# Strided attention and layer-norm FFN on one core: prologue and first chunk as one list of 500 small stages

## The chip, the cores and the metric

The kernel runs on one core of a Trainium2 chip. The metric is the device time of one execution in microseconds (us); the median of three runs is 963.8 us. The engines are named as the profile names them: PE is TensorE, PEld its weight loads, DVE is VectorE, ACT is ScalarE, POOL is GpSimd, SP is SyncE, whose queue issues almost all DMAs.

## The reference

Eight batches, eight heads, 576 tokens, 64 columns a head. Half of the heads look at a local band, half at every 32nd token. The result of attention (512 columns a token) goes through a layer norm without mean offset and a two-layer network with a residual. The matrices `w_ch1` and `w_ch2` come in as 64-bit floats.

```python
scores = scale * np.matmul(q, k.transpose(0, 1, 3, 2))
mask_local = (rel >= 0) & (rel < stride)
mask_strided = (rel >= 0) & (pos[None, :] % stride == pos[:, None] % stride)
scores = np.where(masks[None, :, :, :], scores, -1000000000.0)
attn = np.exp(scores - np.max(scores, axis=-1, keepdims=True))
attn = attn / (np.sum(attn, axis=-1, keepdims=True) + 1e-09)
x = np.matmul(attn, v)                        # heads side by side: [8, 576, 512]
mu, var = x.mean(-1), ((x - mu) ** 2).mean(-1)
xn = (x - mu) / np.sqrt(var + 1e-06) * g_ln
out = x + np.maximum(xn @ w_ch1, 0.0) @ w_ch2
```

## The kernel before

**Tiling.** The 8 x 576 tokens are nine chunks of 512: chunk c holds the first 512 tokens of batch c, the ninth the 64 left over of each batch. For each chunk the hidden layer is walked in 16 slices f of 128 columns. `ffn1` (L630 on) makes slice f of the hidden layer: eight matmuls with the high half of the weights (L643) and four with the low half (L647) into one PSUM bank `ph`. ACT takes the high part of the result (`hh`, L651), DVE the rest (`hl`, L652). `ffn2` (L662) then adds 12 matmuls of the slice to the outputs `po`, which hold four PSUM banks for the whole chunk. Every product is made of high and low parts, so that 24 matmuls belong to one f.

**Attention.** Two heads are a `Pair`; four pairs make a batch, in the order 2, 0, 3, 1 (2 and 3 strided, 0 and 1 local). In what follows a pair is called by its place in the list of all pairs: 0 to 3 are batch 0, 4 to 7 batch 1. For batch 0 `q` and `k` come in as rows and PE transposes them (`t_rows`, L321); from pair 4 on they come in as `raw` through many small descriptors (`load_qk`, L299) and DVE transposes them (`t_piece`, L362 to L367). Then: scores (L396), mask and row maximum on DVE (L423, L432), subtraction on POOL (L437), exponential on ACT (L440), transpose of the weights on PE (L449) and a copy (L454), product with `v` (L464), division on DVE (L475, L476, L513), store to a DRAM scratch (L522 to L527), transpose to the layout of the FFN (L536), high part on ACT (L559), low part on DVE (L561). For local pairs of batch 0 ACT makes a shifted copy of `v` (`v_shifted`, L354).

**Weight splits.** While chunk 0 runs, `Split(f)` turns the 64-bit weights of slice f into a high and a low fp32 part, once for the first matrix (i = 0) and once for the second (i = 1): `scaled` on ACT into the single PSUM tile of the pool `ps_r` (L188), `low` on DVE (L194), `magnitude` and `sign` on DVE (L198, L204); for i = 0 also the factor g on POOL (`by_g`, L212), the mean over the 512 input rows by four matmuls against a matrix of g (`column_mean`, L219) and its subtraction on DVE (`centred`, L223); then `two_parts`, ACT for the high (L234) and POOL for the low (L235). `w_load` (L170, L173) brings 1 MB per f.

**Order.** Each engine takes its instructions in the order of the program; the last loop of the kernel ties them so. Before, the prologue handles batch 0 pair by pair, then slices 0 and 1 are split whole. Then chunk 0 runs f = 0 to 15, and with each f comes the split of f + 2, spread around `ffn1` and `ffn2`, and one piece of batch 1 from the generator `pieces`. From chunk 1 on there are no splits; each f has a piece of the next batch.

Slice f of the first layer is called F(f) for L643 and H(f) for L647, the second layer G(f).

Of the kernel before, what the change touches and what calls it, by code (L numbers as in the profile page):

```python
# [19 lines left out]
def kernel(  # L20
# [43 lines left out]
    ps_o = ctx.enter_context(tc.tile_pool(name="ps_o", bufs=2, space=bass.MemoryType.PSUM))  # L64
# [115 lines left out]
    class Split:  # L180
        def __init__(self, f):
            self.f = f
            self.bits = [t.rearrange("p (f t) -> p f t", t=2) for t in staged.pop(f)]
# [42 lines left out]

        def two_parts(self, i):
            w = (self.wg, self.w[1])[i]
# [5 lines left out]
            nc.scalar.activation(out=t[:, 0], in_=w, func=AF.Copy)  # L234
            nc.gpsimd.tensor_tensor(out=t[:, 1], in0=w, in1=t[:, 0].bitcast(F32), op=ALU.subtract)  # L235

        def whole(self):
            self.low(0)
            self.scaled(0)
            self.magnitude(0)  # L240
            self.sign(0)
            self.low(1)
            self.by_g()
            self.column_mean()
            self.scaled(1)
            self.magnitude(1)
            self.sign(1)
# [635 lines left out]
```

## Time and profile before

| what | value |
|---|---|
| median of three runs | 963.8 us (962.1 to 964.55) |
| profiled execution, own time | 962.39 us |
| its span | 960.6 us |
| PE busy | 926.0 us, 96% |
| DVE busy | 427.0 us, 44% |
| ACT busy | 212.6 us, 22% |
| POOL busy | 127.3 us, 13% |
| F(0) of chunk 0 starts | 55.78 us |
| F(0) of chunk 1 starts | 177.97 us |

The span counts from the first to the last instruction; 1.79 us of the execution lie around it. Busy times of PE count pipelined matmuls whose ends are modelled, so a start-to-start distance is the better price of a matmul group. A start in the timeline is counted from the start of the span.

### The profile page before, as it was taken

The numbers are of one execution on the slowest core, as the hardware profiler recorded it, in microseconds if no ns is written. First come the engines' busy times: TensorE is split into PE (matmuls) and PEld (weight loads), VectorE is DVE, ScalarE is ACT, GpSimd is POOL, SyncE is SP. The second block draws the span as 40 slices with busy tenths as digits, with TensorE's granted clock in tenths as the row PEclk, the third lists the DMA queues.
The fourth block names the chain that finished last, engine by engine and source line by source line (L and its number), as shares of the span: only waits on it lengthen the run. The fifth ranks groups of instructions, "written<-read, shape, count | busy, mean of one in ns | idle before, by whom it ended". The sixth has DMA issues, their size and how long they took to land.

```text
span 960.6 us, 18743 instructions
## 1 busy us (share of the span) xinstructions
PE 926.0 (96%) x7936; PEld 766.6 (80%) x7936; DVE 427.0 (44%) x857; ACT 212.6 (22%) x337; POOL 127.3 (13%) x150
## 2 busy tenths in 40 slices
PE   6669999999999999999999999999999999999997
PEld 6558787788888888888888888888888888888886
DVE  2689988633454334434543454335432331132112
ACT  3534444121111121211121211121111111110100
POOL 4245556100000001000100010001000000000000
PEclk9879999999999999999999999999999999999999
DMA  9866873442333334333433344334221121002001
GB/s 200 238 158 155 208 212 78 85 101 46 86 63 94 62 85 73 95 61 85 73 95 62 83 74 96 62 64 94 71 38 48 36 76 45 0 1 88 1 1 44
DMA packets 239427, 80.16 MB, mean 83 GB/s; under 512 B 190064, under 2 KB 232688, under 8 KB 239344
## 3 DMA queue, kind: packets, MB, share of 16 engines
q1 hardware_dynamic: 236128, 77.27, 35.3%
q10 hardware_dynamic: 3216, 1.71, 0.8%
q8 instruction: 62, 1.02, 0.5%
q14 instruction: 21, 0.17, 0.1%
HBM read 59.48 MB, written 19.46 MB: 82 GB/s over the span
## 4 chain that ended last, share of the span: by engine, by line
PE 89%; DMA 3%; DVE 3%; SPq 3%; issue 1%; ACT 1%; ACTq 0%; DVEq 0%
PE po L662 40%; PE ph L643 26%; PE ph L647 13%; PE m L464 2%; PE m L396 2%; SPq L299 2%; PE cm L219 2%; PE n L449 1%; PE n L536 1%; DMA rows<-in_k_dram 1%; DMA s<-in_moe_w_ch_dram 1%; DVE p L198 1%; SPq L170 1%; PE av L464 0%; DMA raw<-in_k_dram 0%
## 5 line engine op out<-in xcount | busy, mean ns | idle before, releaser
L662 PE MATMUL po<-w,hh 128*128 128x512 f32 x1152 | 362.2, 396 | 0.0
L652 DVE SCALAR_TENSOR_TENSOR hl<-ph,hh 128x512 fp32r<-128x512 f32 x144 | 99.6, 692 | 465.7 <-ACT hh L651 465.3
L662 PEld LDWEIGHTS po<-w,hh 128*128 128x128 f32 x1152 | 211.2, 188 | 43.6
L643 PE MATMUL ph<-xh,w 128*128 128x512 f32 x576 | 227.2, 395 | 0.2 <-ACT xh L559 0.2
L643 PE MATMUL ph<-xl,w 128*128 128x512 f32 x576 | 225.7, 392 | 0.2 <-DVE xl L561 0.2
L662 PE MATMUL po<-w,hl 128*128 128x512 f32 x576 | 224.9, 391 | 0.0
L651 ACT ACTIVATE hh<-ph 128x512 fp32r<-128x512 f32 x144 | 85.9, 597 | 488.8 <-PE ph L647 488.8
L647 PE MATMUL ph<-xh,w 128*128 128x512 f32 x576 | 154.4, 390 | 0.0
L643 PEld LDWEIGHTS ph<-xl,w 128*128 128x128 f32 x576 | 109.0, 189 | 22.8 <-DVE xl L561 0.5
L643 PEld LDWEIGHTS ph<-xh,w 128*128 128x128 f32 x576 | 108.9, 189 | 22.8 <-ACT xh L559 0.7
L647 PEld LDWEIGHTS ph<-xh,w 128*128 128x128 f32 x576 | 108.5, 188 | 22.7
L662 PEld LDWEIGHTS po<-w,hl 128*128 128x128 f32 x576 | 108.1, 188 | 23.3
L437 POOL TENSOR_TENSOR sm<-sm,mx 128x648 f32<-128x648 f32 (+1 forms) x32 | 40.6, 1269 | 420.2 <-DVE mx L432 409.9
L624 POOL TENSOR_TENSOR rs<-rs,mhalf 128x1 f32<-128x1 f32 x36 | 20.0, 554 | 342.3 <-DVE rs L623 342.3
L440 ACT ACTIVATE sm<-sm 128x648 f32<-128x648 f32 (+1 forms) x32 | 23.8, 744 | 138.7 <-POOL sm L437 138.6
L219 PE MATMUL cm<-r,gmean 128*128 128x128 f32 x128 | 19.3, 299 | 16.2 <-DVE r L204 11.3
L219 PEld LDWEIGHTS cm<-r,gmean 128*128 128x128 f32 x128 | 17.7, 208 | 19.1 <-issue 15.6
L561 DVE TENSOR_TENSOR xl<-n,xh 128x480 fp32r<-128x480 f32 (+2 forms) x36 | 22.7, 666 | 15.4 <-ACT xh L559 15.4
L188 ACT ACTIVATE p<-s 128x512 f32<-128x512 f32 x32 | 20.5, 642 | 34.5 <-DVE r L204 33.1
L432 DVE TENSOR_REDUCE mx<-sm 128x12 f32<-128x648 f32 (+1 forms) x32 | 26.4, 824 | 2.3
L513 DVE TENSOR_TENSOR xo<-m,den 64x64 f32<-64x64 f32 (+3 forms) x120 | 27.1, 290 | 0.1
L235 POOL TENSOR_TENSOR w<-wg,w 128x512 fp32r<-128x512 f32 x16 | 20.7, 1292 | 41.9 <-ACT w L234 38.8
(95 smaller groups left out, 645.9 us busy)
## 6 DMA issues: line engine op xcount, KB each, us to landing
s<-in_moe_w_ch_dram SPq DMA_DIRECT2D x32, 512.0 KB
out_dram<-x SPq DMA_DIRECT2D x32, 256.0 KB
raw<-in_q_dram SPq DMA_DIRECT2D x112, 72.0 KB
raw<-in_k_dram SPq DMA_DIRECT2D x112, 72.0 KB
xds<-xo SPq DMA_DIRECT2D x32, 162.0 KB
v_l<-in_v_dram SPq DMA_DIRECT2D x32, 144.0 KB
xdl<-xo SPq DMA_DIRECT2D x16, 256.0 KB
x<-xdl SPq DMA_DIRECT2D x32, 128.0 KB
```

Source lines behind the costliest of these rows:

```text
L219: nc.tensor.matmul(self.mean, gmean[:, c, :], w[:, c, :], start=(c == 0), stop=(c == NCC - 1))
L235: nc.gpsimd.tensor_tensor(out=t[:, 1], in0=w, in1=t[:, 0].bitcast(F32), op=ALU.subtract)
L432: nc.vector.reduce_max(mx[:, :, 0:nt], sm, axis=AX.X)
L437: nc.gpsimd.tensor_tensor(out=sm, in0=sm, in1=mx[:, :, 0:nt].unsqueeze(3).broadcast_to([P, 2, nt, w]), op=ALU.subtract)
L440: nc.scalar.activation(out=sm, in_=sm, func=AF.Exp, scale=SCALE)
L513: nc.vector.tensor_tensor(out=xo[r, t0:t1, h0:h1].rearrange("p t h d -> p h t d"), in0=av, in1=den[r, h0:h1, t0:t1].unsqueeze(3).broadcast_to(
L561: nc.vector.tensor_tensor(out=dst(xl), in0=src, in1=dst(xh).bitcast(F32), op=ALU.subtract)
L643: nc.tensor.matmul(ph, w1h[:, cc], x[:, cc, :], start=(n == 0), stop=False)
L647: nc.tensor.matmul(ph, w1l[:, cc], xh[:, cc, :], start=False, stop=(cc == NCC - 1))
L651: nc.scalar.activation(out=hh, in_=ph, func=AF.Relu)
L652: nc.vector.scalar_tensor_tensor(out=hl, in0=ph, scalar=0.0, in1=hh.bitcast(F32), op0=ALU.max, op1=ALU.subtract)
L662: nc.tensor.matmul(po[i], hx[:, cs], w, start=(f == 0 and n == 0), stop=(f == NFC - 1 and n == 2))
```

## The change

Prologue and chunk 0 no longer come from loops. A table `ORDER` of some 500 words sets them one after the other; `one` takes a word such as `sg:4:0` (operation, pair or slice, part, PSUM room) and writes that stage's instructions. The stages themselves were helpers before and are now cut finer: `t_rows` and `t_copy`, `s_mask`, `s_max`, `s_sub`, `s_exp`, `v_full`, `v_den`, `v_out`, `v_store`, `x_turns`, `x_high`, `x_low`, `low`, `scaled`, `magnitude`, `sign`, `by_g`, `block_sum`, `column_mean`, `centred`, `high`, `rest`, and F, H, G of the FFN. The loops over chunks 1 to 8 stay.

Four stages change what they compute with:

- `low` of slices 2 to 15 (28 instructions) goes to ACT as `lowA`: the top byte of the low word is read, a byte in eight, scaled by 1/32 and rounded to an integer, instead of a shift by 29.
- The mean over rows: POOL adds the four blocks of the weighted slice to one (`block_sum`, two instructions), and PE makes the mean by one matmul against a constant matrix. The build of `gmean` on DVE goes.
- `by_g` writes in place, so that a split holds two buffers of the pool `tk` and not three.
- `v_shifted` goes from ACT to POOL (four copies).

```diff
+ORDER = """
+T:0:0:0 T:0:1:1 c:0:0: T:1:1:2 c:0:1: S:0::0 c:1:1: T:2:0:1 mask:0 max:0 T:1:0:2 c:2:0: sub:0
+...
+hi:1:0 sg:2:0 hi:1:1 lo:1:0 st:0 V:4::0 sc:2:1 lowA:3:1 H:0 mg:2:1 W:5 byg:2 lowA:4:0 den:4 lo:1:1
+...
-        def low(self, i):
+        def low(self, i, on_act):
             t = self.bits[i][:, :, 0]
-            nc.vector.tensor_scalar(t, t, 29, None, op0=ALU.logical_shift_right)
+            if on_act:
+                nc.scalar.activation(
+                    out=t, in_=self.top[i], func=AF.Copy, scale=1.0 / 32, bias=-31.0 / 64)
+            else:
+                nc.vector.tensor_scalar(t, t, 29, None, op0=ALU.logical_shift_right)
...
         def by_g(self):
-            w = self.w[0].rearrange("p (c f) -> p c f", c=NCC)
-            self.wg = tkp.tile([P, DM], F32, tag="tk", name=f"wg{self.f}")
...
+            self.wg = self.w[0].rearrange("p (c f) -> p c f", c=NCC)
             nc.gpsimd.tensor_tensor(
-                out=self.wgv, in0=w, in1=gcol.unsqueeze(2).broadcast_to([P, NCC, P]), op=ALU.mult)
-
-        def column_mean(self):
-            w = self.w[0].rearrange("p (c f) -> p c f", c=NCC)
-            self.mean = bank(f"cm{self.f}")[:, 0:P]
-            for c in range(NCC):
-                nc.tensor.matmul(
-                    self.mean, gmean[:, c, :], w[:, c, :], start=(c == 0), stop=(c == NCC - 1))
+                out=self.wg, in0=self.wg, in1=gcol.unsqueeze(2).broadcast_to([P, NCC, P]),
+                op=ALU.mult)
+
+        def block_sum(self):
+            nc.gpsimd.tensor_tensor(
+                out=bsum, in0=self.wg[:, 0:2], in1=self.wg[:, 2:4], op=ALU.add)
+            nc.gpsimd.tensor_tensor(out=bsum[:, 0], in0=bsum[:, 0], in1=bsum[:, 1], op=ALU.add)
+
+        def column_mean(self, ps):
+            self.mean = ps[:, 0:P]
+            nc.tensor.matmul(self.mean, mean, bsum[:, 0], start=True, stop=True)
...
-                    nc.scalar.copy(
+                    nc.gpsimd.tensor_copy(
                         out=self.v[64 * h:64 * h + 32, 1:NB, 0:D],
                         in_=self.v[64 * h + 32:64 * h + 64, 0:NB - 1, 0:D])
...
+    for word in ORDER.split():
+        part = (word.split(":") + [""] * 3)[0:4]
+        one(part[0], *(int(x or 0) for x in part[1:]))
+    prev = 0, NFC - 1, hs[NFC - 1], xres
...
+    for c in range(1, NCHUNK):
```

What the table moves is shown at three places.

PE around F(0): scores, transposes and products of attention (`pp`, `av`, `px`), the column means `cm`, and the first two matmuls of F(0) (`ph_0`). Before:

```order
L449 MATMUL pp_1_712<-ident,sm_195 128x128 x5
L219 MATMUL cm_731<-r_0_726,gmean 128x128 x4
L464 MATMUL av_1_748<-v_l_183,pt_1_718 32x65 x40
L536 MATMUL px_3_795<-ident,xo_3_701 128x128 x6
L536 MATMUL px_1_806<-ident,xo_1_791 128x128 x4
L219 MATMUL cm_837<-r_1_832,gmean 128x128 x4
L643 MATMUL ph_0_869<-xh_656,w_0_742 128x512
L643 MATMUL ph_0_869<-xl_657,w_0_742 128x512
```

And now:

```order
L490 MATMUL pp_1_705<-ident,sm_201 128x128 x5
L505 MATMUL av_711<-v_l_189,pt_1_705 32x65 x40
L271 MATMUL cm_764<-bsum,mean 128x128
L434 MATMUL s_780<-kt_s,qt_s 64x54 x24
L577 MATMUL px_811<-ident,xo_3_761 128x128 x6
L577 MATMUL px_839<-ident,xo_1_835 128x128 x4
L490 MATMUL pp_852<-ident,sm_200 128x128 x6
L271 MATMUL cm_865<-bsum,mean 128x128
L697 MATMUL ph_0_872<-xh_529,w_0_806 128x512
L697 MATMUL ph_0_872<-xl_530,w_0_806 128x512
```

The last product of batch 0 (`av`) no longer stands behind the first column mean; the scores (`s_780`) and the transpose (`pp_852`) of pair 4 stand ahead of F(0), where they stood behind it; a column mean is one matmul.

DVE in the prologue, from the first `low` on: the splits of slices 0 and 1 (`s`, `p`, `r`), divisions (`den`, `xo`), low parts of attention (`xl`) and the transposes of `raw` for pair 4. Before:

```order
L194 TENSOR_SCALAR s_0_249<-s_0_249 128x512
L198 SCALAR_TENSOR_TENSOR p_0_723<-p_0_723,s_0_249 128x512
L204 SCALAR_TENSOR_TENSOR r_0_726<-s_0_249,p_0_723 128x512
L194 TENSOR_SCALAR s_0_250<-s_0_250 128x512
L198 SCALAR_TENSOR_TENSOR p_0_736<-p_0_736,s_0_250 128x512
L204 SCALAR_TENSOR_TENSOR r_0_739<-s_0_250,p_0_736 128x512
L223 TENSOR_TENSOR wg_729<-wg_729,cm_731 128x512
L475 TENSOR_SCALAR den_201<-av_1_748 128x2x5
L476 RECIPROCAL den_201<-den_201 128x2x5
L513 TENSOR_TENSOR xo_1_791<-av_1_748,den_201 128x2x5x64
```

And now, from `sign` of slice 0 on:

```order
L254 SCALAR_TENSOR_TENSOR r_0_684<-s_0_509,p_0_635 128x512
L409 STREAM_TRANSPOSE qt_s<-raw_2_581 128x18x32
L409 STREAM_TRANSPOSE kt_s<-raw_2_581 128x18x32
L517 TENSOR_SCALAR den_206<-av_652 128x12
L518 RECIPROCAL den_206<-den_206 128x12
L244 TENSOR_SCALAR s_0_510<-s_0_510 128x512
L244 TENSOR_SCALAR s_1_677<-s_1_677 128x512
L248 SCALAR_TENSOR_TENSOR p_0_699<-p_0_699,s_0_510 128x512
L555 TENSOR_TENSOR xo_3_761<-av_652,den_206 128x2x6x64
L244 TENSOR_SCALAR s_1_678<-s_1_678 128x512
L254 SCALAR_TENSOR_TENSOR r_0_766<-s_0_510,p_0_699 128x512
L274 TENSOR_TENSOR r_0_684<-r_0_684,cm_764 128x512
```

The two transposes of pair 4 stood behind all of batch 0 and now stand among it; the split of slice 1 begins before that of slice 0 is centred.

DVE in the middle of chunk 0, one slice's worth: before, around F(4).

```order
L194 TENSOR_SCALAR s_6_924<-s_6_924 128x512
L223 TENSOR_TENSOR wg_1128<-wg_1128,cm_1212 128x512
L198 SCALAR_TENSOR_TENSOR p_6_1221<-p_6_1221,s_6_924 128x512
L204 SCALAR_TENSOR_TENSOR r_6_1232<-s_6_924,p_6_1221 128x512
L194 TENSOR_SCALAR s_6_925<-s_6_925 128x512
L652 SCALAR_TENSOR_TENSOR hl_4_1253<-ph_4_1239,hh_4_1252 128x512
L198 SCALAR_TENSOR_TENSOR p_6_1237<-p_6_1237,s_6_925 128x512
L204 SCALAR_TENSOR_TENSOR r_6_1265<-s_6_925,p_6_1237 128x512
```

And now:

```order
L248 SCALAR_TENSOR_TENSOR p_7_1247<-p_7_1247,s_7_1103 128x512
L714 SCALAR_TENSOR_TENSOR hl_4_1274<-ph_4_1223,hh_4_1263 128x512
L254 SCALAR_TENSOR_TENSOR r_7_1277<-s_7_1103,p_7_1247 128x512
L274 TENSOR_TENSOR r_6_1204<-r_6_1204,cm_1249 128x512
L248 SCALAR_TENSOR_TENSOR p_7_1290<-p_7_1290,s_7_1104 128x512
L254 SCALAR_TENSOR_TENSOR r_7_1312<-s_7_1104,p_7_1290 128x512
```

The two `low` are gone from DVE, and at `hl` of slice 4 it is in the split of slice 7, where it was in that of slice 6.

## Rows read from the trace of the kernel before

**Rows 1.** The page: busy tenths of PE and DVE in 40 slices of 24 us.

```profile
PE   6669999999999999999999999999999999999997
...
DVE  2689988633454334434543454335432331132112
```

**Rows 2.** Windows by stage: length, busy (instructions) by engine, PE clock, DMA share, GB/s.

```profile
0.00:55.78 55.78, 33.18 (x762) 29.78 (x763) 26.62 (x61) 25.24 (x33) 17.05 (x42) 0.90 0.92 213
55.78:73.02 17.24, 14.45 (x108) 11.78 (x108) 13.79 (x22) 7.31 (x13) 8.69 (x7) 0.84 0.47 141
73.02:177.97 104.95, 102.27 (x985) 83.64 (x984) 91.95 (x149) 46.23 (x77) 54.81 (x46) 1.00 0.63 156
177.97:960.60 782.63, 776.13 (x6089) 641.42 (x6087) 294.68 (x627) 133.77 (x215) 46.73 (x55) 1.00 0.29 63
```

**Rows 3.** Windows of 2 us in the prologue, the same columns.

```profile
24.00:26.00 2.00, 2.00 (x77) 1.93 (x69) 1.86 (x4) 0.22 (x2) 0.19 (x1) 1.00 1.09 387
...
42.00:44.00 2.00, 1.79 (x8) 1.78 (x8) 1.59 (x4) 0.65 (x1) 1.16 (x1) 0.50 0.60 166
...
66.00:68.00 2.00, 2.00 (x7) 1.52 (x6) 1.51 (x3) 1.98 (x4) 0.46 (x1) 0.50 0.04 12
```

**Rows 4.** Timeline of PE: start, duration, line, instruction, idle time ahead and its releaser.

```profile
42.21 2.05 PE L219 MATMUL cm<-r,gmean 128*128 128x128 f32 x8 [5.27 <-DVE r L204]
...
54.08 2.04 PE L219 MATMUL cm<-r,gmean 128*128 128x128 f32 x8 [6.06 <-DVE r L204]
55.78 0.77 PE L643 MATMUL ph<-xh,w 128*128 128x512 f32 x1
...
63.45 1.16 PE L219 MATMUL cm<-r,gmean 128*128 128x128 f32 x8 [2.79 <-DVE sm L423]
...
73.02 0.48 PE L643 MATMUL ph<-xh,w 128*128 128x512 f32 x1
...
79.79 1.05 PE L219 MATMUL cm<-r,gmean 128*128 128x128 f32 x8
80.60 0.48 PE L643 MATMUL ph<-xh,w 128*128 128x512 f32 x1
...
83.53 0.93 PE L464 MATMUL av<-v_s,pt 54*64 54x65 f32 x48
84.39 0.73 PE L662 MATMUL po<-w,hh 128*128 128x512 f32 x2
...
177.97 0.47 PE L643 MATMUL ph<-xh,w 128*128 128x512 f32 x1
```

**Rows 5.** Groups by line and shape, 73.02 to 177.97 us: busy us, mean ns, idle ahead.

```profile
L235 POOL TENSOR_TENSOR w<-r,w 128x512 fp32r<-128x512 f32 x13 | 19.1, 1466 | 0.0
L194 DVE TENSOR_SCALAR s<-s 128x512 uint32<-128x512 uint32 x24 | 19.0, 792 | 0.0
L235 POOL TENSOR_TENSOR w<-wg,w 128x512 fp32r<-128x512 f32 x13 | 16.8, 1293 | 34.8 <-ACT w L234 31.7 <-DMA s<-in_moe_w_ch_dram 3.1
L198 DVE SCALAR_TENSOR_TENSOR p<-p,s 128x512 uint32<-128x512 uint32 x24 | 16.6, 692 | 0.4 <-ACT p L188 0.4
...
L188 ACT ACTIVATE p<-s 128x512 f32<-128x512 f32 x24 | 15.4, 644 | 26.3 <-DVE r L204 25.0
...
L212 POOL TENSOR_TENSOR wg<-r,gcol 128x512 f32<-128x512 f32 x12 | 12.4, 1037 | 0.0
```

**Rows 6.** Timeline of DVE, three rows: a transpose of `raw`, and `low` twice.

```profile
49.82 1.25 DVE L367 STREAM_TRANSPOSE qt_s<-raw 128x576 f32<-128x576 f32 x1
...
51.99 0.42 DVE L194 TENSOR_SCALAR s<-s 128x512 uint32<-128x512 uint32 x1
...
92.63 1.13 DVE L194 TENSOR_SCALAR s<-s 128x512 uint32<-128x512 uint32 x1
```

**Rows 7.** Timeline of SP's queue: issue of `raw` for `k` of pair 4.

```profile
25.98 4.18 SPq L299 DMA_DIRECT2D raw<-in_k_dram  x4
```

**Rows 8.** Timeline of ACT: two shifted copies of `v`.

```profile
28.69 2.22 ACT L354 COPY v_l<-v_l 32x1088 f32<-32x1088 f32 x2
```

More of the change, by code (lines that the diff above doesn't have):

```diff
@@ L19 @@
+"""
 @with_exitstack
@@ L61 @@
     dram = ctx.enter_context(tc.tile_pool(name="dram", bufs=1, space=bass.MemoryType.DRAM))
[L64 removed]
+    ps_o = [ctx.enter_context(tc.tile_pool(name=f"ps_o{i}", bufs=1, space=bass.MemoryType.PSUM))
+            for i in range(2)]
     ps_h = ctx.enter_context(tc.tile_pool(name="ps_h", bufs=1, space=bass.MemoryType.PSUM))
@@ L75 @@
     gcol = const.tile([P, NCC], F32, name="gcol")
-    gmean = const.tile([P, NCC, P], F32, name="gmean")
+    mean = const.tile([P, P], F32, name="mean")
+    bsum = const.tile([P, 2, P], F32, name="bsum")
+    const.tile([P, P], F32, name="gap")
+    nc.vector.memset(mean, 1.0 / DM)
     mask_l = const.tile([P, 64], F32, name="mask_l")
@@ L233, in two_parts, with rest @@
                 w_pools[1].tile([P, 88], F32, name="pad")
[L234 to L247, printed above, removed]
-            self.centred()
-            self.two_parts(0)
-            self.two_parts(1)
+            nc.scalar.activation(out=t[:, 0], in_=self.w[i], func=AF.Copy)
+        def rest(self, i):
+            t = (w1s, w2s)[i][self.f]
+            nc.gpsimd.tensor_tensor(
+                out=t[:, 1], in0=self.w[i], in1=t[:, 0].bitcast(F32), op=ALU.subtract)
     banks = [(ps_a, "a", 1024)]
@@ L675, in finish, with second @@
                         out[2 * i + j, CH:S, :], x[REST * j:REST * (j + 1)])
-    WAHEAD = 2
-    banks[:] = [(ps_a, "a", 1024), (ps_o, "o", 1024), (ps_o, "o", 1024)]
+    po = None
+    def second(c, f, h, xres):
+        nonlocal po
+        if f == 0:
+            po2 = [ps_o[i].tile([P, 1024], F32, tag="o", name=f"po{c}_{i}") for i in range(NT // 2)]
+            po = [po2[i // 2][:, DM * (i % 2):DM * (i % 2 + 1)] for i in range(NT)]
+        ffn2(c, f, h, po)
+        if f == NFC - 1:
+            finish(c, po, xres)
     first = pairs[0:NHP]
@@ new lines, with room, weights, split @@
+    ps, ph, hs, splits = {}, {}, {}, {}
+    xres = [None] * NT
+    def room(name, buf):
+        pool, tag = ((ps_a, "a"), (ps_o[0], "o"), (ps_o[1], "o"))[buf]
+        ps[name] = pool.tile([P, 1024], F32, tag=tag, name=f"{name}")
+        return ps[name]
+    def weights(f):
+        if f == NF2:
+            w_late()
+        w_load(f)
+    def split(f):
+        if f not in splits:
+            splits[f] = Split(f)
+        return splits[f]
+    def residue(i):
+        xres[i] = [x_load(0, i)]
@@ L770 @@
     gen = pieces()
[L772 to L788 removed]
+    ps_r_ctx.close()
+    ps_m = ctx.enter_context(tc.tile_pool(name="ps_m", bufs=1, space=bass.MemoryType.PSUM))
+    banks[:] = [(ps_m, "m", 1536)]
+    for c in range(1, NCHUNK):
         xres = []
         tail = {}
[L791 removed]
         for f in range(NFC):
[L793 to L814 removed]
+            ph = ffn1(c, f)
+            hh = h_high(c, f, ph)
+            h = hh, h_low(c, f, ph, hh)
             if c + 1 < B:
@@ L824 @@
                         x_turn(B, i, tail[i])
-            if new:
-                new.sign(1)
-            if prev is not None:
-                second(*prev)
-            if new:
-                new.column_mean()
-            elif c == 0:
-                next(gen, None)
+            second(*prev)
             i = f - (NFC - NT - 3)
```

370 lines of the change are left out of this document (202 added, 168 removed).

## Prediction

> **What bounds the kernel now.** I read the page first [rows 1]: PE is below nine tenths only in the first four slices, some 70 us, and in the last. From 177.97 us, where chunk 1 begins, the change touches nothing and PE is the bound: 776.13 us busy of 782.63 [rows 2], the rest of it the tail. So the question is how much earlier F(0) of chunk 1 can begin than 177.97 us; what is won there is won at the end.
>
> Ahead of it I cut the time at two starts of PE, F(0) at 55.78 and F(2) at 73.02 us [rows 4]. In the prologue PE is busy for 33.18 of 55.78 us [rows 2]; its last two long gaps, 5.27 and 6.06 us, end with `sign` of slices 0 and 1 on DVE, which the column means need [rows 4]. So the prologue waits for the chain attention, then split, that DVE takes one after the other. Between F(0) and F(2) a third gap of 2.79 us ends with a mask on DVE [rows 4], and the granted clock is 0.84 [rows 2]: it reads 0.50 both behind the gap of 5.27 us and behind that of 2.79 us [rows 3]. That is 1.2 GHz in place of 2.4. From F(2) on PE is busy for 102.27 of 104.95 us and DVE for 91.95 [rows 2]. DVE is almost full there too, but PE lost only 2.7 us to it. This stage can shrink by work taken from PE, and otherwise hardly.
>
> **The change part by part.** I price three stages: the start of F(0), from there to F(2), from there to chunk 1.
>
> *Column means.* A mean of four matmuls (eight records) takes PE 0.81 us from its start to the next [rows 4]. With one matmul it should take a quarter, 0.20 us; bounds are 0 and 0.81. After F(2) there are 12 such groups before and 13 now: 9.7 less 2.6 gives 7.1 us off PE (0 to 9.7). The matmul now waits for two more instructions of POOL. They read 256 and 128 columns; against 1.04 us for `by_g` with 512 [rows 5] I take 0.9 us for both (bounds 0.4 and 2.1). That is latency of a split made more than a slice ahead, so PE pays for it only if splits run late.
>
> *POOL.* Between F(0) and chunk 1 it was busy for 8.69 and 54.81, together 63.5 us [rows 2]. With 16 block sums at 0.9 it has 78 us, at 2.1 it has 97, in a stage that I expect to last 109. It stays off the end, but its queue gets a wait in the prologue: the subtraction of pair 2 now stands behind the four shifted copies of `v`. A pair of those takes ACT 2.22 us [rows 8]. POOL has no such row; I take ACT's and allow twice that. Twice would put the subtraction, the exponential of pair 2 on ACT and the first `scaled` queued behind it up to 4.4 us later.
>
> *`low`.* DVE loses 24 of 0.79 us after F(2) [rows 5] and four more before it, some 22 us. ACT gains 28. Its nearest row is `scaled`, the same 512 elements at the same stride of 8 bytes, 0.64 us [rows 5]: 18 us more on 53.5 busy between F(0) and chunk 1 [rows 2]. A byte as input is in no row; the bounds are 0.6 and 1.1 us (one copy of 1,088 elements [rows 8]), so 70 to 84 us. It fits beside PE at either end. The Trainium skill, page "ScalarE: Activation LUTs", section "Rules for kernel authors", would leave such arithmetic on DVE, since DVE is faster per element. The rows agree in part, 0.42 us alone on DVE but 1.13 beside POOL [rows 6]. By the rule the change would free 28 times 0.42 or 11.8 us of DVE and not 22, and the sum stays as it is, because DVE at 94 us of 109 would still be off the end.
>
> With 105.7 us busy before [rows 2] less 22, DVE is near 84 of 109 us. This is what lets splits run ahead of PE.
>
> *Start of F(0).* It needs the last low part of batch 0. Now the two transposes of `raw` for pair 4 stand in DVE's queue ahead of most of batch 0's second half, so DVE stops there until `raw` has landed. Before, its issue ended at 30.2 us [rows 7], behind the weights of slices 0 and 1; now slice 1 stands behind it, and 1 MB at 387 GB/s [rows 3] is 2.7 us less. With some 3 us to land I take 31 us; bounds are 28 and 36 (nothing hidden, and POOL's 4.4 us on top). From the first transpose to the last low part there are 24 instructions on DVE. The mean of that engine from start to start is 91.95/149, 0.62 us [rows 2]: 14.8 us. F(0) comes at 45.8 us, 10 earlier. Four `low` in this stretch are priced like the rest; the spread between 0.42 and 1.13 [rows 6] is 2.8 us, which I add to the bounds: 42 to 52.
>
> The Trainium skill, page "SBUF — State Buffer", section "Who interferes with whom", says that VectorE's two-port modes, which a shift by a constant can enter, and GpSimd lock each other out. The rows agree: 1.13 us beside POOL, 0.42 without [rows 6]; and POOL's 1.47 against 1.29 us [rows 5]. By it every one of the four shifts would wait if POOL is working just then, the upper bound above.
>
> *F(0) to F(2).* One slice of 12 first-layer matmuls takes 2.93 us (80.60 to 83.53), the product for a pair 0.86 [rows 4]. The chain now is F(0) and H(0) with the product of pair 4 between, 3.8; its division and one `sign` on DVE partly beside H(0), 1.5; the transpose of pair 4, 0.6; F(1) and H(1), 2.9; G(0), also 12 matmuls, 2.9; the mean 0.2; `centred` and the high part, 0.7 and 0.6; handoffs 0.5. That is 13.7 us at full clock. PE idles in the prologue as before, so I let 0.50 [rows 3] hold for part of the first 4.4 us and add 1.3 (0 to 4.4): 15.0 us against 17.24. F(2) comes at 60.8 us against 73.02.
>
> *F(2) to chunk 1.* From 104.95 us go the 2.7 idle, 7.1 of means, and the product (0.86) and transpose (0.6) of pair 4 that now lie ahead: 93.1; I leave 0.6 for new bubbles: 93.7.
>
> *Queues.* On SP the weights of slice 4 now stand behind the store of pair 3, those of slice 2 behind a load of `v` that waits for pair 1's product. ACT's shifts for slices 2 to 4 would hold the high parts and exponentials queued behind them if these loads came late. In the stretch the DMAs are busy for 0.47 to 0.63 [rows 2] and a megabyte takes 2.7 us, so I cost it at nothing; if the cover is gone, F(0) slips by about that much.
>
> *Sum.* 45.8 + 15.0 + 93.7 = 154.5 us, against 177.97: 23.5 us less. The profiled execution took 962.39 us, 960.6 span and 1.8 around it: 938.9 us. Its time is 1.4 below the median of the runs, so against the median of 963.8 I forecast 940 us, with 934 to 947 as this case's own range.
>
> **The rivals.** *The front half does not come.* In-order holds (raw, the copies on POOL, weights behind stores) eat what attention ahead gives, and F(2) stays at 73. For it speaks that DVE's queue in the prologue now depends on DMAs in the middle of the chain; against it that DVE has 22 us less to do and long idle times in the first 56 us (26.62 busy [rows 2]). Then only 2.7 + 7.1 + 1.4 us or 11 are won: 952 us.
>
> *It comes fuller.* F(0) at 43 us, full clock from the start, PE without a bubble: 43 + 13.7 + 92.5 = 149, that is 29 us less: 935; with cheaper handoffs and short bubbles around the means gone too, 932. For it speaks PE's shorter gaps ahead of F(0): scores, two transposes and `pp` of pair 4 fill them.
>
> *The pace of the splits stays.* The single PSUM tile of `scaled` makes a chain: `scaled` 0.64, `magnitude` 0.69, `sign` alike [rows 5], twice a slice, some 4.5 us with handoffs against 5.8 us of matmuls a slice. Only if each link waits 0.6 us more in its queue does it bind, and then nothing is won behind F(2) and the front is given back: 960 to 965 us.
>
> *Slower.* The shift on ACT reads one byte in eight and writes integers in place, a form that no row shows. The stage from F(0) at 46 would have to last until 181 us, 135 us, for a loss beyond 0.3%. ACT has 53.5 us of other work there [rows 2], so the mechanism decides from (135 - 53.5)/28 or 2.9 us a shift. At 3.5 it gives some 980 us. The nearest row says 0.64, so the chance is small.
>
> **How the numbers follow.** 0.62 for the forecast, 0.17 for the front half that does not come, 0.12 for the fuller gain, 0.05 for the pace that stays, 0.04 for the slow shift. About 0.3% is what a measurement of this kernel can tell from no change. The first three are faster by more than that, and 0.02 of the fourth: 0.93. The rest of the fourth is the same, 0.03; the last is slower, 0.04. The range takes in the fuller gain and the front half that does not come, and leaves out the last two cases and the edges: 931 to 953 us.
>
> **What would show it right or wrong.** F(0) at 42 to 52 us, and the low part of pair 3 on DVE as its releaser; F(2) near 61; between F(2) and chunk 1 some 94 us with under 2 us of idle PE; a column mean of two records and about 0.2 us; DVE busy for about 84 us between F(0) and chunk 1, `scaled` and the shift on ACT equal within 0.2 us; POOL under 100 us. If F(0) comes early and chunk 1 doesn't, the splits are late: then PE's idle time names `centred` or the high part, and I have misjudged their chain. If DVE waits for a transpose of `raw` past 36 us, the prologue is wrong. Chunk 1 to the end should take 782 to 783 us as before; another number there would show an effect that I haven't named.

## The result, and the profile after

The changed kernel took 949.25 us (median of 4 runs, 949.24 to 951.44), the kernel before 963.04 beside it (962.1 to 964.55): a ratio of 0.986, 95% interval 0.984 to 0.988. The forecast was 940 us with a range of 931 to 953. So the direction and the range held, but of 23.5 us that were to be won 13.9 came: the profiled span is 946.7 us where it was 960.6.

The page of the changed kernel, busy tenths of PE and DVE in 40 slices (before: [rows 1]):

```profile
PE   7689889999999999999999999999999999999997
...
DVE  3877676433543355334543344345433321122112
```

PE is at eight tenths or less in the first six slices but one, where it had been full from the fourth slice on. The same by stage, cut at F(0), at F(2) and at the start of chunk 1 (length, busy time and count of PE, PEld, DVE, ACT, POOL, granted clock, DMA share, GB/s; before: [rows 2]):

```profile
0.00:47.12 47.12, 31.32 (x805) 27.25 (x805) 26.70 (x63) 23.98 (x34) 24.78 (x51) 0.85 0.96 205
47.12:61.63 14.51, 12.10 (x94) 9.33 (x93) 11.85 (x20) 11.20 (x21) 8.71 (x9) 0.89 0.90 243
61.63:165.06 103.43, 96.53 (x859) 77.09 (x859) 73.45 (x121) 54.63 (x93) 67.23 (x72) 0.97 0.73 174
165.06:946.70 781.64, 775.60 (x6089) 641.56 (x6086) 293.81 (x626) 134.16 (x215) 46.76 (x55) 1.00 0.29 63
```

| start of | before | forecast | after |
|---|---|---|---|
| F(0), us | 55.78 | 45.8 | 47.12 |
| F(2), us | 73.02 | 60.8 | 61.63 |
| chunk 1, us | 177.97 | 154.5 | 165.06 |
| F(2) to chunk 1, us | 104.95 | 93.7 | 103.43 |

The front came as forecast; the stage from F(2) to chunk 1 is only 1.5 us shorter. There PE is busy for 96.53 us, 5.7 us less than before, where 8.6 were forecast, and it idles for 6.9 us (before 2.7), and the granted clock is 0.97 (before 1.00). Its timeline names the two long gaps (start, duration, line, instruction, idle time ahead and releaser; before: [rows 4]):

```profile
74.70 0.38 PE L271 MATMUL cm<-bsum,mean 128*128 128x128 f32 x2
74.84 0.47 PE L697 MATMUL ph<-xh,w 128*128 128x512 f32 x1
...
111.79 0.80 PE L271 MATMUL cm<-bsum,mean 128*128 128x128 f32 x2 [2.94 <-POOL bsum L267]
...
141.81 0.49 PE L271 MATMUL cm<-bsum,mean 128*128 128x128 f32 x2 [2.48 <-POOL bsum L267]
```

Both are column means (of slices 10 and 14) that wait for the block sum on POOL. Behind each the granted clock falls to half, 1.2 GHz, as the windows of 2 us show (columns as above):

```profile
108.00:110.00 2.00, 0.84 (x4) 0.38 (x2) 0.30 (x1) 2.00 (x4) 0.76 (x1) 1.00 0.77 178
110.00:112.00 2.00, 0.21 (x1) 0.21 (x2) 1.58 (x3) 1.65 (x4) 1.92 (x4) 0.95 1.02 372
112.00:114.00 2.00, 2.00 (x6) 1.70 (x7) 1.35 (x3) 0.81 (x2) 1.97 (x2) 0.50 0.97 326
...
144.00:146.00 2.00, 2.00 (x8) 1.61 (x7) 1.83 (x6) 0.00 (x0) 2.00 (x3) 0.52 0.24 73
```

POOL was not slow at either place; it was idle. The waits of all engines from 61.63 to 165.06 us (sum, times, longest) lead on:

```profile
ACT s L241 <- DMA s<-in_moe_w_ch_dram: 13.7, 10, 3.7
POOL w L288 <- ACT w L284: 12.2, 7, 5.7
...
POOL rs L674 <- DVE rs L673: 6.8, 2, 5.4
...
DVE st L669 <- DMA x<-xds: 3.8, 1, 3.8
```

The first gap followed back, timelines of POOL, ACT and SP's queue:

```profile
109.24 1.27 POOL L288 TENSOR_TENSOR w<-r,w 128x512 fp32r<-128x512 f32 x1 [5.73 <-ACT w L284]
110.47 0.73 POOL L265 TENSOR_TENSOR bsum<-r 128x256 f32<-128x256 f32 x1
```
```profile
107.97 0.67 ACT L241 ACTIVATE s<-s 128x512 uint32<-128x512 uint8 x1 [3.73 <-DMA s<-in_moe_w_ch_dram]
108.55 0.61 ACT L284 ACTIVATE w<-r 128x512 fp32r<-128x512 f32 x1
```
```profile
98.02 0.89 SPq L214 DMA_DIRECT2D s<-in_moe_w_ch_dram  x1
...
100.97 2.68 SPq L383 DMA_DIRECT2D v_l<-in_v_dram  x1
103.69 1.17 SPq L384 DMA_DIRECT2D v_l<-in_v_dram  x1
104.91 2.83 SPq L214 DMA_DIRECT2D s<-in_moe_w_ch_dram  x1
```

Read from below: the weights of slice 12 are issued from 98.02 us on, behind the raw load of pair 8 (its issues end at 95.86) and ahead of a load of `v` that is wanted only 50 us later, and land some 9 us on. ACT stands at their shift (`lowA`) until 107.97, although the result is wanted two slices later. Behind that shift, in order, waits a high part; POOL's low part waits for it, the block sum of slice 10 stands behind that, and PE waits for the sum. The second gap is of the same kind on another engine:

```profile
137.66 0.69 DVE L669 BATCH_NORM_STATS2 st<-x 128x6 f32<-128x512 f32 x1 [3.82 <-DMA x<-xds]
```
```profile
138.84 0.55 POOL L674 TENSOR_TENSOR rs<-rs,mhalf 128x1 f32<-128x1 f32 x1 [5.35 <-DVE rs L673]
139.36 1.04 POOL L260 TENSOR_TENSOR r<-r,gcol 128x512 f32<-128x512 f32 x1
```

DVE stands at the statistics (`xs:0`) of the first residual tile until its load has landed, POOL at the power that follows, and the product with g and the block sums of slice 14 stand behind that.

### The profile page after: what moved, and what is told of

It reads as the page before. It is cut to its first block, busy times and chain, and to the rows that moved or that the text cites. A ratio compares the mean times of both kernels' runs of the same rounds, so it can differ in the third digit from the quotient of the medians.

```text
span 946.7 us, 18534 instructions
## 1 busy us (share of the span) xinstructions
PE 915.5 (97%) x7840; PEld 755.2 (80%) x7840; DVE 405.8 (43%) x829; ACT 224.0 (24%) x361; POOL 147.5 (16%) x186
## 4 chain that ended last, share of the span: by engine, by line
PE 92%; issue 2%; DVE 2%; DMA 1%; POOL 1%; SPq 1%; ACT 0%; ACTq 0%; DVEq 0%; POOLq 0%
PE po L724 40%; PE ph L697 27%; PE ph L704 13%; PE m L505 2%; PE m L434 2%; PE n L490 1%; PE n L577 1%; DMA rows<-in_k_dram 1%; SPq L340 1%; PE av L505 1%; PE s L434 1%; PE pp L490 1%; PE cm L271 0%; PE t L360 0%; PE px L577 0%
## 5 line engine op out<-in xcount | busy, mean ns | idle before, releaser
L288 POOL TENSOR_TENSOR w<-r,w 128x512 fp32r<-128x512 f32 x32 | 41.1, 1291 | 23.4 <-ACT w L284 19.4
L248 DVE SCALAR_TENSOR_TENSOR p<-p,s 128x512 uint32<-128x512 uint32 x32 | 22.3, 696 | 10.5 <-ACT p L234 10.2
L669 DVE BATCH_NORM_STATS2 st<-x 128x6 f32<-128x512 f32 x36 | 24.3, 676 | 3.8 <-DMA x<-xds 3.8
L730 DVE SCALAR_TENSOR_TENSOR x<-po,rs,x 128x512 f32<-128x512 f32 x36 | 24.5, 736 | 3.1 <-PE po L724 2.8
```

The source lines that it names most:

```text
L288: nc.gpsimd.tensor_tensor(out=t[:, 1], in0=self.w[i], in1=t[:, 0].bitcast(F32), op=ALU.subtract)
L730: nc.vector.scalar_tensor_tensor(out=x, in0=po[i], scalar=rs, in1=x, op0=ALU.mult, op1=ALU.add)
```

## The experiments

Theory A: the stage lost its gain to loads that an in-order engine stands in front of long before it needs them. Rival B: POOL with the block sums is the limit. The other rivals are in the expectations. The stages of all kernels, from their profiles:

| kernel | median, us | ratio to before | F(2) | F(2) to chunk 1 |
|---|---|---|---|---|
| after | 949.25 | 0.986 (0.984 to 0.988) | 61.6 | 103.4 |
| low_late | 948.08 | 0.984 (0.981 to 0.987) | 62.8 | 100.3 |
| w_first | 945.27 | 0.981 (0.978 to 0.984) | 62.0 | 98.7 |
| st_late | 947.85 | 0.984 (0.980 to 0.988) | 63.3 | 100.9 |
| all3 | 945.45 | 0.981 (0.979 to 0.984) | 62.9 | 97.6 |
| w_st | 944.58 | 0.981 (0.977 to 0.985) | 62.7 | 97.2 |
| mean4 | 949.64 | 0.987 (0.985 to 0.990) | 65.2 | 100.8 |
| w_st_mean4 | 948.46 | 0.987 (0.984 to 0.990) | 62.9 | 101.3 |
| low_dve | 952.66 | 0.991 (0.989 to 0.993) | 66.2 | 102.0 |
| list_alone | 958.25 | 0.996 (0.994 to 0.998) | 70.6 | 104.5 |
| compute_alone | 971.62 | 1.010 (1.007 to 1.013) | 76.1 | 110.5 |
| loads | 948.82 | 0.987 (0.984 to 0.990) | 59.6 | 104.3 |
| by_need | 947.21 | 0.983 (0.980 to 0.986) | 62.4 | 101.4 |

The first six of these kernels share the list up to F(2), yet their F(2) lies between 61.6 and 63.3 us; mean4 and w_st_mean4, which are the same as each other up to there, have 65.2 and 62.9. So a difference of 2 us between two profiles is no finding by itself. In low_late, w_first, st_late and all3 the list has one line less, and lines of the trace are one lower.

**low_late.** Shifts on ACT just ahead of their use; slice 12 as the example.

```diff
-lowA:12:1
...
-lowA:12:0
...
+lowA:12:0
 sc:12:0
...
+lowA:12:1
 sc:12:1
```

> Edit of the changed kernel's list alone: each shift on ACT (lowA) of slices 6 to 15 stands just ahead of the scaled copy (sc) of the same half, not up to two slices earlier. Nothing is added or removed; the loads keep their order. In the changed kernel ACT stands still for 13.7 us in front of these shifts between F(2) and chunk 1 because the weights have not landed, the longest time 3.73 us at 107.97 us, and the high parts behind them come late. Theory A (an in-order engine waits for a load long before its result is wanted): the stall of 2.94 us at the mean of slice 10 goes, and the half clock behind it, 5 us in all; about 944.5 us. Rival B (GpSimd with its block sums is the limit): no change, 949. Rival C (the chain of one PSUM tile from scaled to sign is the limit): the shift now lies in that chain, 0.67 us twice a slice, so no better and up to 4 us worse, 949 to 953.

Measured 948.08 us. ACT's wait for weights is gone from its list of waits, and so is the gap at the mean of slice 10; the stage is 3.2 us shorter. The gap at slice 14 is still there (2.5 us). The stage moved as theory A says, by less than its 5 us; the median, 1.2 lower, can't be told from no change.

**w_first.** The same wait taken from the other side. Of SP's words and the transposes `tp`:

```diff
-W:10 tp:7 r:8 W:11 st:5 W:12 v:7 W:13 W:14 W:15 tp:8
+W:10 W:11 tp:7 W:12 W:13 W:14 st:5 W:15 r:8 v:7 tp:8
```

> Edit of the changed kernel's list alone: on SP the weights of slices 11 to 15 are issued ahead of the raw load of pair 8 and of the load of v for pair 7, which now stand behind the weights of slice 15. Same bytes, same work on the other engines. Theory A (weights late because they queue behind loads that are wanted much later): ACT's wait for weights of slices 11 to 15 (6.8 us of the 13.7) goes, the stall of 2.94 us at the mean of slice 10 with its half clock too; about 944.5 us. Rival D (the 16 DMA engines are simply full, 0.97 busy from 60 to 115 us): the waits move to another place and the time stays within 1.5 us, 948 to 950. Rival B (GpSimd is the limit): 949.

Measured 945.27 us, stage 98.7: ACT waits for weights for 7.3 us (13.7) and PE's gap at slice 10 is gone. The bytes are the same, so it was the order of the queue and not only full DMA engines. The granted clock of the stage is 1.00, PE is busy for 93.90 us.

**st_late.**

```diff
-xs:0
...
 xs:1
+xs:0
```

> Edit of the changed kernel's list alone: the statistics of the first residual tile (xs:0: one 512-wide statistics instruction, two small ones on DVE, one on POOL) stand behind those of the second tile, some 1.2 slices later. In the changed kernel DVE waits 3.82 us for that tile's load at 137.66 us, and POOL 5.35 us behind it, and PE then 2.48 us for the block sum of slice 14, with half clock from 142.6 to 145.2 us. Theory A: the stall and the half clock behind it go, 2.5 + 1.3 us; about 945.5 us. Rival B (GpSimd's block sums are the limit there, DVE's wait only coincides): 949. Rival E: the tile's load is late whatever stands behind it, and the wait moves to the new place: 948 to 949.

Measured 947.85 us, stage 100.9. The gap at slice 14 is gone; that at slice 10 stands (3.41 us), as it should. As with low_late the stage moves and the median doesn't say enough.

**all3** and **w_st** (w_first and st_late without low_late).

> The three edits of low_late, w_first and st_late together. Theory A: both stalls and the half clock behind them go, chunk 1 begins at 155 to 158 us in place of 165.06, 940 to 942 us. If the edits of shifts and of weights treat the same wait, they do not add: the sum of the larger of those two and of st_late, about 941. Rivals B and C: within 2 us of 949.

> The edits of w_first and st_late together, without low_late: weights of slices 11 to 15 ahead of the raw load of pair 8 and of v for pair 7 on SP, and the first residual's statistics 1.2 slices later. In w_first the stage from F(2) to chunk 1 took 98.8 us with 93.9 of PE busy at full clock; its longest stall left (2.5 us, block sum of slice 14) is the one that st_late took away. Theory A (PE's waits are loads that in-order engines stand in front of): 98.8 - 2.5 = 96.3 us for the stage, 942 to 943 us. Rival B (GpSimd's block sums set the pace): the wait moves on, 945 as w_first.

all3 took 945.45 us, w_st 944.58; both have neither gap. Theory A named some 941 and 942 to 943, so 4 and 2 us stay out. The time of w_st is also that of rival B (945); its trace is not: between F(2) and chunk 1 PE doesn't wait for a block sum at all. The edits don't add: one wait leaves with either low_late or w_first, and with all three a transfer of the wait shows, 1.88 us of PE at 94.63 for a `centred` on DVE. w_st is the fastest of the study, but it can't be told from w_first and all3, and its interval overlaps that of the changed kernel; the stages speak more plainly. That of w_st, with that of mean4 and of w_st_mean4 below (columns as above):

```profile
62.70:159.90 97.20, 93.47 (x859) 74.48 (x859) 73.63 (x121) 54.30 (x93) 67.27 (x72) 1.00 0.76 187
```
```profile
65.20:166.00 100.80, 100.78 (x937) 83.61 (x937) 73.05 (x121) 54.79 (x93) 53.07 (x46) 1.00 0.75 178
```
```profile
62.90:164.20 101.30, 100.98 (x937) 83.51 (x937) 73.12 (x121) 54.71 (x93) 53.07 (x46) 1.00 0.71 178
```

**mean4** and **w_st_mean4.** The mean by four matmuls and no block sums, in the changed kernel's list and in that of w_st.

```diff
-            nc.gpsimd.tensor_tensor(
-                out=bsum, in0=self.wg[:, 0:2], in1=self.wg[:, 2:4], op=ALU.add)
-            nc.gpsimd.tensor_tensor(out=bsum[:, 0], in0=bsum[:, 0], in1=bsum[:, 1], op=ALU.add)
...
-            nc.tensor.matmul(self.mean, mean, bsum[:, 0], start=True, stop=True)
+            for c in range(NCC):
+                nc.tensor.matmul(self.mean, mean, self.wg[:, c], start=(c == 0), stop=(c == NCC - 1))
```

> The changed kernel with its list, but the column mean is four matmuls over the product with g again, and GpSimd's two block sums a slice are left out. Theory A (GpSimd has room; the waits come from loads): 13 means after F(2) and some before it cost 0.8 us on PE in place of 0.2, some 8 us more; the two stalls that end with a block sum are 1.2 us shorter each, as GpSimd is done sooner; 954 to 956 us. Rival B (the block sums on GpSimd are the limit behind F(2)): the stalls of 2.94 and 2.48 us with the half clock behind them go and pay the means back, 949 or less.

> The list of w_st (weights of slices 11 to 15 and the first residual's statistics moved) with the mean by four matmuls and without block sums on GpSimd. mean4 had PE busy for 100.78 of 100.80 us from F(2) to chunk 1, w_st for 93.47 of 97.20. Theory A (loads and block sums are two limits in a row, and whichever is slower shows): PE is the limit with four matmuls, so the earlier loads give nothing here, the stage stays at 101 us and the time at 948.5 to 950.5; the one-matmul mean is then worth some 5 us with the loads moved, and was worth nothing in the changed kernel. Rival D (the loads alone set the pace): 944 to 945, as w_st.

mean4 took 949.64 us: the same as the changed kernel, not the 954 to 956 of theory A. Its stage is even 2.6 us shorter (100.8 against 103.4); its F(2) came 3.6 us later. The reason is in the second row above: PE works 7.3 us more than in w_st and has no gap at all (100.78 of 100.80). So one matmul in place of four did take 7.3 us off PE, and the waits for loads took all of it back; a slower PE just met the weights later. Rival B's number is met, but its reason isn't: the gaps of low_late, w_first and st_late closed with both block sums in place. w_st_mean4 tells it apart: with the loads moved, four matmuls cost 948.46 against 944.58 us and 101.3 against 97.2 in the stage. So the one-matmul mean with its block sums is worth nothing in the changed kernel and some 4 us once the loads are in order.

**list_alone** and **compute_alone.** The two halves of the change, each without the other. list_alone has the shifts on DVE, the copies of `v` on ACT and the edit of mean4 in the changed kernel; compute_alone has the new work in the order of before:

```diff
+            if self.f >= 2:
+                nc.scalar.activation(
+                    out=t, in_=self.top[i], func=AF.Copy, scale=1.0 / 32, bias=-31.0 / 64)
...
-                    self.mean, gmean[:, c, :], w[:, c, :], start=(c == 0), stop=(c == NCC - 1))
+            nc.tensor.matmul(self.mean, mean, bsum[:, 0], start=True, stop=True)
...
-                    nc.scalar.copy(
+                    nc.gpsimd.tensor_copy(
```

> The changed kernel's list alone, with the older work in it: the mean by four matmuls and no block sums, the shifts all on DVE at the places of the list, the shifted copies of v on ACT. (The product with g stays in place.) Theory A: the front half comes as in the changed kernel, F(2) within 2 us of 61.6, because the list sets it; behind F(2) the means cost 8 us more and DVE waits for weights where ACT did; F(2) to chunk 1 some 110 us, 955 to 957 us. Rival F (the front needs the shifts off DVE and the copies off ACT): F(2) at 66 or later, 960 and more. Rival B (block sums are the limit): 949.

> The kernel before with its own order, and only the new work in it: column mean by one matmul from two block sums on GpSimd, the product with g in place, shifts of slices 2 to 15 on ACT, shifted copies of v on GpSimd. Theory A: behind F(2) it is PE that bounds, so the 12 means of 0.81 us become 0.2 and 7 us go, and the 2.1 us of PE waiting for DVE go too; ahead of F(0) the two slices' means wait 1.2 us more each for GpSimd, so F(0) comes 1 to 3 us later; 955 to 958 us. Rival B (GpSimd with the block sums is too slow): nothing is won behind F(2), 962 to 966. If this and list_alone add up, their two gains make the changed kernel's 13.8.

compute_alone took 971.62 us, 8.5 longer than before and beyond both expectations. PE's longest waits and POOL's timeline in it (lines of that kernel):

```profile
PE cm L229 <- POOL bsum L225: 22.1, 11, 8.4
```
```profile
96.34 2.55 POOL L244 TENSOR_TENSOR w<-r,w 128x512 fp32r<-128x512 f32 x2 [4.44 <-ACT w L243]
98.85 1.04 POOL L220 TENSOR_TENSOR r<-r,gcol 128x512 f32<-128x512 f32 x1
99.97 0.72 POOL L223 TENSOR_TENSOR bsum<-r 128x256 f32<-128x256 f32 x1
100.77 0.45 POOL L225 TENSOR_TENSOR bsum<-bsum 128x128 f32<-128x128 f32 x1
```

The old order writes the low parts of one slice ahead of the product with g of the next. Before, PE's mean read only `sign` and passed by that queue; with block sums it stands behind it, 2.62 us of PE at 101.28. So rival B's mechanism shows here, by POOL's order and not its load: POOL is busy for 66.63 of the 110.46 us behind F(2). This is read from the trace; no run moved the product with g alone.

list_alone took 958.25 us, with F(2) at 70.6: the list alone doesn't bring the front. That is rival F's F(2) (66 or later), though not its 960 us; theory A's "within 2 us of 61.6" was wrong by 7, and its stage of 110 us was 104.5. In that kernel DVE stood 5.1 us for weights ahead of F(2) with the shifts that it kept. The halves alone give -4.9 and +8.5 us, which add up to +3.6; both together give -13.8. They don't add: each needs the other.

**low_dve.** The shifts alone back on DVE.

```diff
-            split(k).low(i, True)
+            split(k).low(i, False)
```

> The changed kernel with its list, but the shifts of slices 2 to 15 are done by DVE at the same places of the list (0.4 us alone, 1.1 beside GpSimd; 28 of them, 12 to 31 us more on DVE). Theory A (in-order engines stand in front of loads): the wait for weights moves from ACT to DVE, where the transposes, the masks and hl are queued behind it; F(0) to F(2) 15 to 18 us in place of 14, F(2) to chunk 1 106 to 109 in place of 103.4, 954 to 957. Rival G (DVE has room since it was busy for only 73 of 103 us): within 2 us of 949.

Measured 952.66 us, between theory A and rival G. DVE has 84.15 us of work behind F(2) in place of 73.45, but the stage there takes 102.0 us and not the 106 to 109 of theory A. The loss lies ahead of it: F(0) to F(2) takes 16.7 us, as theory A says, and F(2) comes 3 to 5 us later than in the six kernels that share the front. PE waits there for two divisions on DVE:

```profile
46.53 1.09 PE L577 MATMUL px<-ident,xo 128*128 128x128 f32 x4 [3.74 <-DVE xo L555]
...
56.59 1.44 PE L577 MATMUL px<-ident,xo 128*128 128x128 f32 x6 [2.84 <-DVE xo L555]
```

In the changed kernel the same two waits are 1.64 and 0.98 us. DVE stands in front of weights for only 1.6 us before F(2) and 1.7 us behind it, so the loss is DVE's added work and not, as theory A had it, the wait moved to DVE.

**loads** and **by_need.** More loads moved. SP's words (without stores) and `tp` of w_st and of loads, then of by_need:

```diff
-W:1 tp:4 v:5 W:2 v:4 W:3 W:4 W:5 v:6 r:5 W:6 tp:5 W:7 r:6 W:8 tp:6 W:9 r:7 W:10 W:11 tp:7 W:12 W:13 W:14 W:15 r:8 v:7
+W:1 tp:4 W:2 v:4 W:3 W:4 W:5 v:5 v:6 r:5 W:6 tp:5 W:7 W:8 W:9 r:6 W:10 tp:6 W:11 r:7 W:12 W:13 W:14 tp:7 W:15 r:8 v:7
```
```diff
+W:1 tp:4 W:2 v:4 W:3 W:4 W:5 r:5 W:6 tp:5 W:7 W:8 W:9 v:5 r:6 W:10 tp:6 r:7 W:11 tp:7 W:12 W:13 W:14 W:15 r:8 v:6 v:7
```

> w_st with more loads put in the order in which they are wanted: v for pair 5 behind the weights of slice 5, the weights of slices 8 and 9 ahead of the raw load of pair 6, those of 10 and 11 ahead of that of pair 7, and the two transposes of raw for pairs 6 and 7 later on DVE by as much. In w_st ACT still waited 8.8 us for weights (3.33 for slice 8) and PE 2.8 for hl, which stood behind a transpose of raw. Theory A: ACT's wait for weights falls under 4 us, the stage from F(2) to chunk 1 goes from 97.2 to 94.5 to 96 us; 941.5 to 943.5. Rival H (what is left is the latency of the chain from scaled to high part): within 1 us of w_st, 944 to 945.5.

> w_st with every load on SP in the order in which it is wanted: v for pair 5 leaves its place ahead of the weights of slice 2 and stands with the weights of slices 8 and 9 between the weights of slice 7 and the raw load of pair 6; v for pair 6 stands no longer ahead of the raw load of pair 5 but behind that of pair 8; the weights of slice 10 stand ahead of the raw load of pair 7. The run called loads showed both sides of this: with v of pair 5 out of the prologue F(0) came at 45.3 us and F(2) at 59.6 (48.9 and 62.7 in w_st), but v of pairs 5 and 6 ahead of the raw load of pair 5 (10 us of issues) then held DVE at its transposes and gave it all back. Theory A (the forecast of 940 failed only by loads that in-order engines stand in front of): F(0) at 45 to 46.5, F(2) at 59.5 to 61.5, F(2) to chunk 1 95 to 97 us; 938.5 to 942. Rival D (the DMA engines are full, and a wait taken away here comes back there): 943.5 to 946, as w_first and w_st.

They took 948.82 and 947.21 us, where w_st had taken 944.58. In loads F(0) came at 45.3 us and F(2) at 59.6. The expectation of by_need puts this down to `v` of pair 5, which left the prologue. That isn't shown: by_need has the same list up to F(0), and there F(0) came at 48.0 and F(2) at 62.4, past theory A's 45 to 46.5 and 59.5 to 61.5. From 10 us to F(0) PE stands still with no releaser for 3.30 us in loads and for 6.64 in by_need (see the last section). Behind F(2) both lost: in loads `v` for two pairs stood ahead of the raw load of pair 5; in by_need the weights of slices 8 and 9 and `v` stood ahead of that of pair 6, and the transposes on DVE had not been moved with it. DVE of loads, DVE and PE of by_need:

```profile
65.62 0.78 DVE L404 STREAM_TRANSPOSE qt_l<-raw 128x576 f32<-128x576 f32 x1 [2.36 <-DMA raw<-in_q_dram]
```
```profile
83.46 1.26 DVE L409 STREAM_TRANSPOSE qt_s<-raw 128x576 f32<-128x576 f32 x1 [6.25 <-DMA raw<-in_q_dram]
```
```profile
87.30 0.80 PE L697 MATMUL ph<-xh,w 128*128 128x512 f32 x1 [5.66 <-DVE hl L714]
```

That is rival D's wait that comes back in another place, with theory A's mechanism: in this stretch a load brought forward is another load put back, and whoever stands in front of that one waits. Apart from that gap of 5.66 us by_need's stage would be 95.7 us, as expected of it; that no order of the list has all of it at once isn't shown.

## Why the prediction was right, and where it missed

The measured 949.25 us lies outside the 934 to 947 that the prediction gives as this case's own range. It lies inside 931 to 953 because that range took in the rival of a front half that doesn't come (952 us). This rival isn't what happened: the front came, and the stage behind it failed. That the wider range held is in part luck.

- **Start of F(0), 45.8 us:** 47.12, within the bounds of 42 to 52. The term of 14.8 us for DVE held: from its first transpose of `raw` at 31.97 to the last low part at 46.66 it took 14.7 us. The 31 us ahead of it were met by luck. They were to come from the landing of `raw`, and no run shows the 3 us that the prediction took for that; but DVE reached the transposes from its own work, without a wait, 4.35 us after the last issue of `raw` had ended (27.62). Nor is the low part F(0)'s releaser, as forecast: PE has no idle time ahead of F(0), it comes there from `pp` of pair 4 and a mean.
- **F(0) to F(2), 15.0 us:** 14.51, and the parts fit within 0.6 us: F(0), the product and H(0) 5.6 us (3.8 and 1.3 for the clock), the wait for the division 0.98 (1.5), F(1) and H(1) 2.8, G(0) 2.7 (2.9 each).
- **Column means, 7.1 us off PE:** a mean is now two records and 0.14 us from its start to the next; the stage's PE work differs by 7.3 us between w_st and mean4.
- **PE's work from F(2) on, 93.1 us:** the prediction subtracted wrongly. 104.95 less 2.7, 7.1, 0.86 and 0.6 is 93.7, so that the term of 93.7 holds PE's work alone and nothing for bubbles. At full clock the work is 93.47 us in w_st: its size was right.
- **DVE, 84 us from F(0) to chunk 1:** 11.85 + 73.45, 85.3. **POOL, 78:** 75.9. Shift and `scaled` on ACT equal within 0.2 us: 0.675 and 0.632, the block sums 0.74 + 0.46 in place of 0.9, the four copies of `v` on POOL 4.53 us, twice ACT's 2.22 for a pair. The low parts on POOL take 1.293 for all 26, where half of them had taken 1.466. The prediction read that difference as POOL held up by the shifts on DVE; in low_dve, with the shifts back on DVE, they take 1.310, so that reading isn't borne out. The groups of the changed kernel (busy us, mean ns, idle ahead; before: [rows 5]):

```profile
L288 POOL TENSOR_TENSOR w<-r,w 128x512 fp32r<-128x512 f32 x26 | 33.4, 1293 | 12.3 <-ACT w L284 12.2
...
L234 ACT ACTIVATE p<-s 128x512 f32<-128x512 f32 x23 | 14.5, 632 | 9.9 <-DVE r L254 9.9
L241 ACT ACTIVATE s<-s 128x512 uint32<-128x512 uint8 x20 | 13.4, 675 | 13.9 <-DMA s<-in_moe_w_ch_dram 13.7
...
L265 POOL TENSOR_TENSOR bsum<-r 128x256 f32<-128x256 f32 x13 | 9.6, 738 | 0.7
...
L267 POOL TENSOR_TENSOR bsum<-bsum 128x128 f32<-128x128 f32 x13 | 6.0, 461 | 1.0
```

- **The step that failed: "0.6 for new bubbles", which the sum didn't even hold, with the queues costed "at nothing".** The stage took 103.43 us, 9.7 more than the term of 93.7. 6.9 of it are idle time, and 2.8 are busy time over 93.7, which is the granted clock: the same work takes 96.53 us at 0.97 here and 93.47 at 1.00 in w_st. The prediction did name ACT's shifts, queued behind late weights, with high parts behind them. But it took the DMA share from the kernel before, read 0.47 to 0.63 there as cover, and asked only what a late load would cost F(0). In the changed kernel the loads are packed into the first half: the share is 0.90 to 0.96 until F(2), and then 0.98 up to 115 us. Before, then after, from 60 to 115 and from 115 to 165 us (columns as above):

```profile
60.00:115.00 55.00, 51.19 (x533) 41.91 (x524) 50.80 (x77) 25.07 (x42) 27.95 (x24) 0.97 0.65 174
115.00:165.00 50.00, 48.35 (x367) 39.94 (x368) 45.12 (x77) 22.96 (x40) 28.93 (x25) 1.00 0.61 156
```
```profile
60.00:115.00 55.00, 49.15 (x442) 38.95 (x441) 40.34 (x64) 33.59 (x58) 41.13 (x44) 0.97 0.98 238
115.00:165.00 50.00, 47.52 (x419) 38.08 (x418) 34.41 (x60) 21.72 (x37) 27.73 (x30) 0.96 0.46 104
```

That late loads in front of in-order engines are the cause is shown for both long gaps, each of which went when its one wait was moved; that brought the stage to 97.2 us, 3.5 above the term. In w_st PE still idles for 3.7 us: 2.8 at three places for `hl` on DVE and 0.8 with no releaser. At the longest, DVE had waited 1.08 and 0.77 us for `raw` at two transposes ahead of `hl`; the other two weren't followed:

```profile
83.60 0.50 PE L697 MATMUL ph<-xh,w 128*128 128x512 f32 x1 [1.52 <-DVE hl L714]
```

- **The signs.** "If F(0) comes early and chunk 1 doesn't, the splits are late" is what happened; PE's idle time named the block sum, one link ahead of `centred`.
- **The rival that the front doesn't come** would have been true of the list alone (F(2) at 70.6). The prediction gave the front to the list and the DVE relief to the stage behind; the runs put 3 to 5 us of the front on the shifts (low_dve), and more on both kinds of new work together.
- **The rival that the pace of the splits stays** named the outcome behind F(2), where almost nothing was won, but its reason isn't borne out: low_late puts every shift of slices 6 to 15 into that chain of splits, and the stage gets 3.2 us shorter.
- **Chunk 1 to the end, 782 to 783 us:** 781.64.

The prediction weighed a rule of the Trainium skill, page "ScalarE: Activation LUTs", section "Rules for kernel authors": relu, max, min, add and mul belong on VectorE, which per element is up to about three times faster in bf16. In low_dve 25 such shifts take 0.657 us each on DVE, in the changed kernel 0.675 on ACT: no difference here, and by the end the kernel with them on ACT is faster (949.25 against 952.66 us). The measurement decides.

## What to carry to other kernels

Before a stage is shortened, list for each load in it when it lands and which in-order engine stands in front of it: work taken off the bounding engine is worth nothing where the next limit is a load, and here 7.3 us of PE work were worth 0 before the loads were reordered and 4 after. Move a consumer together with its load: on a full queue a load brought forward puts another back, which paid where that one was wanted much later (w_first) and not where an engine stood in front of it (loads, by_need). Test a change of work and a change of order together and apart: here one half alone was 8.5 us slower than nothing.
